# Batch 0's w_out product in split form, 24 matmuls of zeros ahead of TensorE's queue, and a new list of steps up to the first pair

## The chip, the cores and the metric

The kernel runs on one core of a Trainium2 chip. The metric is the device time of one execution in microseconds (us), lower is better. TensorE (PE) multiplies matrices, VectorE (DVE), ScalarE (ACT) and GpSimd (POOL) work on elements, and SyncE (SP) issues all transfers (DMA).

## The reference

Three stages follow one another. The first is an attention between 512 tokens and 32 state vectors per head, in both directions; the second a gated block with layer norm; the third a two-layer block. Cut to what matters:

```python
# x: [8 batches, 8 heads, 512, 64], state: [8, 8, 32, 64]
scores  = scale * x @ state.T;  a  = softmax(scores);  xread = a  @ state
scores2 = scale * state @ x.T;  a2 = softmax(scores2); sread = a2 @ x
x = concat([xread, sread]) as rows of 512        # 8 * (512 + 32) = 4608 rows
h = x @ w_in                                      # 512 -> 1024
solu = h * softmax(h)
ln = (solu - mean) / sqrt(var + 1e-6) * g_ln      # over the 1024
x = ln @ w_out                                    # 1024 -> 512
h = x @ w_in2;  g = max(0.01 * h, h);  out = g @ w_out2   # 512 -> 2048 -> 512
```

The weights come as 64-bit floats; the kernel narrows them itself.

## The kernel before, in words

**Stages.** Batches are worked on one by one through the first two stages. Per batch b: x is loaded (`x`), state is loaded (`z`) and transposed (`Z`), x is transposed (`T`), scores and their softmax run in both directions (`S`, `U`), the second direction is transposed and multiplied with x (`A`, `R`), the first is transposed (`B`). State times w_in is formed once (`Y` for batches 0 and 1, `W` for later pairs), so that `h` is the softmax times that product, followed by softmax, product and layer norm over 1024 columns. `t` transposes the result, four blocks to a PSUM bank, and `X` multiplies it with w_out into the rows of the next stage, which go to DRAM. The rows of `sread` of all batches are treated once, as a ninth batch (`G`, `N`, `t8`, `X8`). Behind that the third stage runs over pairs of batches: the first pair (`H`, `O`, with the ninth batch in `K`, `Q`) prepares the weights chunk by chunk, and the other three pairs follow a pattern that is repeated (`rest`, line 1253, token `F`). There the weights of w_out2 for later pairs are formed by GpSimd out of a loaded tile `wf` (`part_wo2`, line 766).

**Split form and plain form.** A product in split form takes each operand as a rounded high part and the rest as a low part, both of type fp32r, and adds three matmuls (`mm3`): high by high, high by low, low by high. In plain form (`mm1`) it is one fp32 matmul, which the trace shows as two records. `PLAIN_S = (0, 1)` names the batches whose attention and `h` are plain; `PLAIN_L = (0,)` (line 32) the batches whose product with w_out is plain. For those `tr` (line 563) writes one fp32 tile with a ScalarE copy per bank; for the others `split` makes a ScalarE cast to the high part and a VectorE subtraction for the low part. The product itself is `x2` (line 592). The plain one reads the narrowed w_out (`w_out_f`), the split one reads `w_out_hi` and `w_out_lo`, which `split_w_out` (tokens `p`, line 279) forms with a ScalarE cast and a GpSimd subtraction for each quarter.

**Narrowing.** `narrow` (line 198) turns a quarter of w_in (tokens `i`) or of w_out (tokens `o`, `narrow_w_out` in line 267) from 64 into 32 bits: one ScalarE step and four VectorE steps of 128x1024. w_out's quarters are then scaled by g_ln on ScalarE.

**Buffers.** The ring `ln` has four large buffers. They hold first the raw w_in (two) and the raw w_out (two); a buffer that comes free takes w_out_f, and later the transposed layer norm, two for a batch in split form and one in plain form. The four one-bank PSUM tiles are a ring too (`bank`), as are the three row buffers (`row`). x has one buffer `xn`, so x of the next batch can be loaded only behind `R` of the one before.

**The order.** It is written out by hand in `PROGRAM` (line 1356): a list of tokens, each of which advances one of the small generators above by one step (`stage`, line 1312). The first token `T0.0` issues the transposes, the second the eviction, and so on. Everything issued through `InOrder` keeps this order on its engine, and on SyncE's queue for transfers; so a step that waits holds back whatever stands behind it on the same engine. Only `make_identity`, which uses the engine directly, is not pinned. Constants are set by GpSimd ahead of the list (lines 153 to 178): the identity `ident`, `nhalf`, the zeroed state tiles `z0`, `z1`, the tile `stq` (128x2048, high and low part of the transposed state) and `stp`.

Of the kernel before, what the change touches and what calls it, by code (L numbers as in the profile page):

```python
# [64 lines left out]
def attn_solu_leaky_kernel(  # L65
# [1297 lines left out]
    Z2.0 h0.1 Y1.0.1 h0.1 Y1.0.1 o2 T1.0 h0.0 o0 T1.0 h0.1 h0.1 z3. T1.1 T1.1 h0.0 Z2.1 o2 S1.0
    h0.0 T1.2 T1.3 T1.2 S1.0 S1.0 T1.3 h0.0 h0.0 S1.0 S1.1 S1.0 S1.1 S1.1 h0.1 h0.0 U1.1 h0.2
    S1.1 h0.0 o0 h0.3 S1.0 U1.1 Z2.1 U1.0 U1.1 h0.0 h0.3 S1.1 h0.1 S1.1 U1.0 U1.0 h0.1 A1.0 A1.0
    A1.1 A1.1 h0.0 j1 t0.0.0 t0.0.0 U1.1 U1.1 h0.2 h0.1 t0.1.0 h0.3 t0.0.1 U1.0 U1.0 t0.1.0 h0.3
    h0.2 h0.3 j3 t0.0.1 R1 R1 B1.0 Z3.0 B1.1 h0.3 h0.2 h0.2 t0.1.1 h0.2 t0.1.1 h1.2 x2. R1 h0.3
    h0.3 h0.3 Z2.1 Z3.0 Z3.0 h1.2 h0.2 h1.0 R1 h0.3 t0.3.1 Z3.0 Z2.1 Z2.1 Z3.0 h0.2 t0.3.0 T2.2
    o3 T2.0 t0.3.1 h0.2 t0.3.0 T2.0 h0.2 t0.2.0 T2.1 h1.2 t0.2.0 o3 T2.0 T2.1 T2.1 o3 h1.0 h1.0
    p1 T2.2 t0.2.1 t0.2.1 T2.3 T2.2 j3 h1.2 T2.3 S2.0 S2.0 X0.1 h1.2 X0.1 h1.2 Z3.1 j0 j0 T2.3  # L1370
    S2.0 S2.1 h1.3 h1.0 Z3.1 h1.0 h1.0 S2.1 h1.1 j1 z4. S2.1 S2.1 o3 h1.1 h1.2 j1 h1.2 S2.0 Z3.1
    U2.1 W1.0.0 S2.1 o3 W1.0.1 h1.3 o3 o2 X0.1 U2.1 W1.0.0 j0 W1.0.1 h1.0 S2.0 U2.0 h1.3 W1.0.1
    X0.1 Z3.1 Z3.1 X0.1 w1.3 W1.0.0 X0.2 h1.3 h1.1 h1.0 X0.2 W1.1.0 W1.0.0 W1.0.1 W1.0.1 h1.0
    W1.0.0 W1.1.0 U2.0 h1.3 W1.3.1 U2.0 U2.1 W1.1.0 W1.1.0 X0.2 X0.2 X0.1 X0.0 X0.0 h1.2 W1.3.1
    W1.3.1 X0.2 X0.2 W1.3.1 h1.3 h1.3 h1.2 h1.0 t1.0.0 W1.3.1 U2.1 t1.0.0 t1.0.1 t1.0.0 z5. h1.1
    p1 S2.0 h1.1 X0.0 W1.1.0 U2.1 t1.0.1 X0.0 t1.0.1 U2.0 X0.0 S2.1 W1.3.0 W1.3.0 W1.3.0 U2.0
    X0.3 A2.0 A2.1 W1.3.0 W1.3.0 X0.3 A2.1 h1.3 t1.2.0 W1.1.1 A2.0 W1.1.1 h1.1 p2 h1.3 t1.2.1
    W1.1.1 t1.2.1 p3 X0.3 X0.3 h1.1 W1.1.1 B2.0 t1.2.0 t1.2.1 X0.0 w1.2 X0.3 h1.3 B2.1 R2 R2 x3.
    h1.1 B2.0 t1.2.0 B2.0 R2 B2.1 h1.1 W1.2.0 h1.1 W1.2.0 W1.1.1 B2.1 X0.3 t1.1.0 W1.2.1 W1.2.1
    R2 t1.3.0 t1.1.0 W1.2.0 t1.1.0 t1.3.0 W1.2.1 W1.2.0 W1.2.0 h2.2 W1.2.1 h2.1 W1.2.1 t1.3.1  # L1380
# [142 lines left out]
```

## Time and profile before

| | us |
|---|---|
| median of three runs | 1156.82 (1155.01 to 1158.55) |
| profiled execution, its own time | 1156.16 |
| its span, first to last instruction | 1154.4 |
| TensorE busy | 1128.9 (98%) |
| VectorE busy | 895.7 (78%) |
| ScalarE busy | 540.7 (47%) |
| GpSimd busy | 540.2 (47%) |

A span is measured within the profiled execution; its own time has some 1.8 us around the span. Busy time is a union of instructions; the mean of a group counts each instruction from its start to its end, and the next may start a little before that end. Tile names in a row stand as output<-inputs: `st` scores, `xt` transposed x, `zt` transposed state, `sw` and `sv` state times w_in, `h` and `e` the gated block, `tr` and `ln` its transposes, `x` the product with w_out, `wi`, `wo`, `wn` weights that are being narrowed.

### The profile page before, as it was taken

The page shows a single profiled execution, that of the slowest core. Times are in us where ns is not written, and L with a number is a line of the kernel's source. Part 1 is how long each engine was busy: PE and PEld are TensorE (multiplying, and loading weights), DVE is VectorE, ACT ScalarE, POOL GpSimd, SP SyncE. Part 2 cuts the span into 40 slices and gives each one's busy share as a digit, 9 for nine tenths or more (in the row PEclk, how much of TensorE's full clock was granted, in tenths as well). Part 3 has the DMA queues.
Part 4 walks back from the last instruction along what each step waited for, and adds up shares of the span by engine and source line. Part 5 has one row for each costly group of instructions (what it writes and reads, how often), then busy time and mean ns, then how long its engine had stood idle before and what let it go on. Part 6 is the DMA issues. An engine that isn't in the chain of part 4 may idle for free.

```text
span 1154.4 us, 16468 instructions
## 1 busy us (share of the span) xinstructions
PE 1128.9 (98%) x6192; PEld 945.8 (82%) x6192; DVE 895.7 (78%) x1406; ACT 540.7 (47%) x907; POOL 540.2 (47%) x411
## 2 busy tenths in 40 slices
...
GB/s 317 93 107 136 55 96 64 139 19 92 152 70 108 130 162 155 246 210 131 243 208 202 183 346 220 289 238 229 318 292 273 179 278 254 236 222 236 148 192 74
DMA packets 88376, 211.85 MB, mean 184 GB/s; under 512 B 41320, under 2 KB 49512, under 8 KB 79080
## 3 DMA queue, kind: packets, MB, share of 16 engines
...
## 4 chain that ended last, share of the span: by engine, by line
PE 89%; DMA 4%; DVE 3%; issue 1%; POOL 1%; ACT 0%; POOLq 0%; SPq 0%; DVEq 0%; ACTq 0%
PE x L51 17%; PE hX L51 14%; PE oX L51 10%; PE h L51 10%; PE o L51 8%; PE hY L51 7%; PE oY L51 5%; PE hZ L51 3%; PE tr L51 3%; PE sr L51 2%; PE oZ L51 2%; PE st L51 2%; PE sv L51 1%; DVE C L51 1%; PE sw L51 1%
## 5 line engine op out<-in xcount | busy, mean ns | idle before, releaser
L51 DVE TENSOR_TENSOR oacc<-oacc,oX 128x512 f32<-128x512 f32 x171 | 116.2, 683 | 52.9 <-PE oX L51 51.0
L51 PE MATMUL x<-ln,w_out_hi 128*128 128x512 f32 (+1 forms) x512 | 153.8, 384 | 0.0
L51 PE MATMUL hX<-xbT,w 128*128 128x512 f32 x576 | 149.9, 395 | 1.5 <-ACT C L51 1.2
L51 ACT COPY C<-hX 128x512 f32<-128x512 f32 x96 | 56.4, 587 | 171.1 <-PE hX L51 171.0
L51 PEld LDWEIGHTS hX<-xbT,w 128*128 128x128 f32 x576 | 103.4, 188 | 21.3 <-ACT C L51 1.6
L51 PEld LDWEIGHTS x<-ln,w_out_hi 128*128 128x128 f32 x512 | 92.2, 188 | 17.6
L51 PE MATMUL h<-sw,a1T 128*128 128x512 f32 x352 | 103.6, 436 | 0.0
L51 PE MATMUL x<-ln,w_out_lo 128*128 128x512 f32 (+1 forms) x256 | 97.2, 380 | 0.0
L51 POOL TENSOR_TENSOR gc<-C,gc 128x512 fp32r<-128x512 f32 (+1 forms) x43 | 69.3, 1614 | 50.2 <-ACT gc L51 25.5
L51 POOL TENSOR_TENSOR gb<-C,gb 128x512 fp32r<-128x512 f32 (+1 forms) x43 | 69.8, 1629 | 45.9 <-ACT gb L51 23.6
L51 DVE SCALAR_TENSOR_TENSOR C<-C 128x512 f32<-128x512 f32 (+1 forms) x88 | 82.7, 940 | 0.6
L51 PEld LDWEIGHTS h<-sw,a1T 128*128 128x128 f32 x352 | 64.1, 188 | 23.2 <-issue 11.0
L51 DVE TENSOR_TENSOR C<-C,hY 128x512 f32<-128x512 f32 x64 | 43.9, 686 | 43.7 <-ACT C L51 35.2
L51 DVE TENSOR_TENSOR oacc<-oacc,oY 128x512 f32<-128x512 f32 x93 | 63.3, 683 | 2.7 <-PE oY L51 2.0
L51 DVE TENSOR_TENSOR oacc<-oacc,o 128x512 f32<-128x512 f32 x70 | 45.7, 681 | 21.6 <-PE o L51 21.3
L51 PEld LDWEIGHTS x<-ln,w_out_lo 128*128 128x128 f32 x256 | 48.1, 188 | 9.8
L51 DVE TENSOR_TENSOR ln<-tr,ln 128x512 fp32r<-128x512 f32 x60 | 40.4, 684 | 17.9 <-ACT ln L51 17.5
L51 POOL TENSOR_TENSOR gb<-S,gb 128x512 fp32r<-128x512 f32 x27 | 44.6, 1656 | 16.8 <-ACT gb L51 8.1
L51 ACT CAST ln<-tr 128x512 fp32r<-128x512 f32 x60 | 34.5, 588 | 35.3 <-PE tr L51 35.2
L51 PE MATMUL hX<-xbB,w 128*128 128x512 f32 x192 | 50.9, 401 | 0.0
L51 POOL TENSOR_TENSOR gc<-S,gc 128x512 fp32r<-128x512 f32 x26 | 39.3, 1521 | 24.6 <-ACT gc L51 12.7
L51 PE MATMUL hY<-xbB,w 128*128 128x512 f32 x192 | 49.7, 394 | 0.4 <-DVE C L51 0.4
(696 smaller groups left out, 2801.8 us busy)
## 6 DMA issues: line engine op xcount, KB each, us to landing
...
```

What stands on the lines that cost most here:

```text
L51: done = call(*args, **kw)
```

## The change

It sets `PLAIN_L` to nothing: batch 0's product with w_out runs in split form as that of all others, and its transposed layer norm takes two `ln` buffers. It puts 24 matmuls of zeros, 128x512 of type fp32r into one PSUM bank, in front of TensorE's queue; they read the first quarter of `stq`, whose zeroing is moved ahead of the rest, while the identity, `nhalf` and the rest of `stq` are set behind. And `PROGRAM` is written anew from its first token to the start of `F`. In the new list the load of g_ln is the first transfer, the first two loads of w_in precede state, both others precede the second state, and x of batch 0's second half comes behind these; two `Y0.0` steps stand in front of `T0.2` and `T0.3`; the splits of w_out (`p`) stand in front of `X0.1` or within it; the order of the other steps differs in most places.

```diff
+WARM = 24
 PLAIN_S = (0, 1)
-PLAIN_L = (0,)
+PLAIN_L = ()
...
     ident = slot("ident", [P, P], F32, "ident")
-    make_identity(tc.nc, ident)
     nhalf = slot("nhalf", [P, 1], F32, "nhalf")
-    nc.gpsimd.memset(nhalf, -0.5)
...
     stq = slot("q7", [P, 2, NHP, 4 * BLK], F32R, "stq")
-    nc.gpsimd.memset(f32(stq), 0.0)
+    nc.gpsimd.memset(f32(stq[:, 0, :2, :]), 0.0)
+    warm = bank("warm")
+    zeros = stq[:, 0, :2, :].rearrange("p a b -> p (a b)")
+    for _ in range(WARM):
+        nc.tensor.matmul(warm, zeros[:, :P], zeros, start=True, stop=True)
+    drop("warm")
+    make_identity(tc.nc, ident)
+    nc.gpsimd.memset(nhalf, -0.5)
+    nc.gpsimd.memset(f32(stq[:, 0, 2:, :]), 0.0)
+    nc.gpsimd.memset(f32(stq[:, 1]), 0.0)
...
-            raws["w"] = slot(take("ln", "w_out_f", 4 + ND), [P, NF, DM], F32, "w_out_f")
+            raws["w"] = slot(take("ln", "w_out_f", 4 + ND * len(PLAIN_L)), [P, NF, DM], F32, "w_out_f")
...
 PROGRAM = """
-    a0 i0 i0 i0 i0 i0 z0. Z0.1 a1 x0.0 T0.0 Z0.0 a3 i1 i1 i1 Z0.0 Z0.0 z1. i1 T0.0 i1 T0.1 T0.1
-    a2 S0.0 x0.1 i3 Z0.1 Z1.1 i2 Z1.1 Z0.1 T0.3 Z1.1 T0.2 Y0.0.0 i3 i3 i3 T0.3 z2. i2 i2 i2 T0.2
-    i2 Z1.0 S0.1 Y0.0.0 S0.0 S0.0 Z1.0 Z1.0 j2 j2 b0 i3 S0.1 S0.1 o0 U0.0 U0.1 S0.0 b2 b3 o2
...
+    g a0 i0 i0 i0 a1 x0.0 T0.0 z0. i1 T0.0 T0.1 Z0.0 Z0.0 i0 a3 i0 a2 Z0.1 z1. T0.1 i1 i1 Z0.1
+    i1 Z0.1 i1 x0.1 z2. Z0.0 i3 i2 b0 b1 i3 b2 b3 i3 S0.0 S0.0 S0.0 S0.0 Y0.0.1 Y0.0.1 Z1.0 i3
+    Y0.0.0 i2 T0.2 i3 i2 Z1.0 T0.2 S0.0 i2 T0.3 T0.3 S0.1 U0.0 Z1.0 i2 Y0.0.0 Z1.1 S0.1 Y1.0.1
...
```

(The last lines are cut; some 2,100 tokens are in another order.)

## Rows read from the trace of the kernel before

**Rows 1.** The page, part 1: busy time, share of the span, instructions.
```profile
PE 1128.9 (98%) x6192; PEld 945.8 (82%) x6192; DVE 895.7 (78%) x1406; ACT 540.7 (47%) x907; POOL 540.2 (47%) x411
```

**Rows 2.** TensorE's waits in the span: us in total, times, longest.
```profile
PE zt L51 <- DMA z<-in_state: 6.9, 1, 6.9
PE xt L51 <- DMA xn<-in_x: 5.3, 5, 2.3
PE oX L51 <- POOL gc L51: 3.4, 2, 3.1
```

**Rows 3.** The chain of waits up to 180 us: start, us, what.
```profile
6.97 6.92 DMA raw_in<-in_moe_w_in
...
14.31 4.62 DMA xn<-in_x
...
76.18 1.41 PE st L51 x6
...
90.78 6.87 PE x L51 x16
...
141.30 8.40 PE x L51 x36
```

**Rows 4.** One stretch: length, busy of PE, PEld, DVE, ACT, POOL, clock, DMA.
```profile
7.17:78.00 70.83, 66.78 (x271) 38.81 (x271) 67.47 (x120) 49.01 (x94) 13.58 (x14) 1.00 0.57 171
```

**Rows 5.** Groups by form, 0 to 440 us: busy, mean ns, idle before.
```profile
L51 DVE TENSOR_TENSOR ln<-tr,ln 128x512 fp32r<-128x512 f32 x58 | 39.0, 684 | 15.9 <-ACT ln L51 15.6
...
L51 DVE SCALAR_TENSOR_TENSOR wi<-raw_in,wi 128x1024 uint32<-128x1024 uint32 x4 | 4.9, 1226 | 0.1
...
L51 POOL TENSOR_TENSOR w_out_lo<-w_out_f,w_out_hi 128x1024 fp32r<-128x1024 f32 x4 | 9.6, 2390 | 2.6 <-ACT w_out_hi L51 2.6
```

**Rows 6.** The timeline, 0 to 80 us: start, us, engine, operation, idle before.
```profile
1.74 1.81 POOL L51 MEMSET stq<- 128x2048 f32 x1
...
12.86 3.75 PE L51 MATMUL st<-xT_hi,stp 128*128 128x512 f32 x4 [0.17 <-issue]
...
16.76 1.20 ACT L51 ACTIVATE wi<-raw_in 128x1024 f32<-128x1024 f32 x1 [1.60 <-DMA raw_in<-in_moe_w_in]
...
21.40 1.88 PE L51 MATMUL st<-xT_hi,stp 128*128 128x512 f32 x4
...
45.06 1.22 DVE L51 SCALAR_TENSOR_TENSOR e(0, 1)_386<-h,e(0, 1)_386 128x1024 f32<-128x1024 f32 x1
46.20 0.09 DVE L51 DVE_READ_ACCUMULATOR e(0, 1)_386<-h,e(0, 1)_386 128x1 f32 x1
...
73.65 1.46 DVE L51 SCALAR_TENSOR_TENSOR xT_lo<-xt,xT_hi 128x512 fp32r<-128x512 f32 x2
```

**Rows 7.** SyncE's issue of g_ln, then two stretches as in rows 4.
```profile
20.22 0.53 SPq L51 DMA_DIRECT2D gln<-in_moe_g_ln  x1
...
24.00:26.00 2.00, 2.00 (x6) 0.93 (x5) 2.00 (x5) 1.30 (x4) 2.00 (x1) 1.00 1.04 426
...
30.00:32.00 2.00, 2.00 (x12) 1.44 (x11) 1.90 (x6) 2.00 (x4) 1.05 (x1) 1.00 1.15 363
```

**Rows 8.** The timeline near x of batch 4: SyncE's issues, TensorE.
```profile
165.68 0.92 SPq L51 DMA_DIRECT2D wi<-wsc  x2
168.84 7.42 SPq L51 DMA_DIRECT2D xn<-in_x  x4
...
181.15 1.20 PE L51 MATMUL xt<-ident,xn 128*128 128x128 f32 x9 [1.93 <-DMA xn<-in_x]
```

**Rows 9.** The hand-over: GpSimd's timeline, the chain, one stretch.
```profile
693.14 0.74 POOL L51 TENSOR_TENSOR wd<-wf 128x256 f32<-128x256 f32 x1 [8.55 <-DMA wf<-wf2s]
...
699.88 2.56 PE hX L51 x6
...
701.00:703.00 2.00, 2.00 (x8) 1.71 (x7) 2.00 (x3) 0.53 (x2) 2.00 (x2) 0.52 1.06 453
```

**Rows 10.** A group by form, 440 to 680 us, columns as in rows 5.
```profile
L51 DVE SCALAR_TENSOR_TENSOR wn<-raw,wn 128x1024 uint32<-128x1024 uint32 x28 | 41.9, 1503 | 0.5
```

More of the change, by code (lines that the diff above doesn't have):

```diff
@@ L1363 @@
[L1363 to L1380, printed above, removed]
@@ new lines @@
+    A1.0 A1.1 U1.1 t0.1.0 h0.2 t0.1.0 U1.0 U1.1 t0.1.1 U1.0 t0.1.1 t0.1.1 t0.0.0 R1 h0.3 R1
+    t0.0.0 h0.3 h0.3 Y1.0.0 h0.2 Z3.0 U1.0 R1 B1.1 B1.0 Y1.0.0 h0.2 h0.2 R1 j2 h0.3 x2. t0.0.1
+    t0.0.1 t0.0.1 o3 h0.2 h1.0 t0.1.0 o3 p1 h1.2 Z3.0 Z3.0 o3 Z3.0 h0.3 h0.3 Z3.0 p0 T2.0 T2.3
+    T2.1 T2.3 T2.1 j3 o3 h0.3 h0.2 h0.2 T2.3 h1.2 t0.3.0 h0.2 p2 T2.1 p2 t0.3.0 t0.3.0 T2.2 T2.2
+    T2.2 j2 h1.0 Z2.0 t0.2.0 S2.1 T2.0 T2.0 Z2.0 j0 j0 Z2.0 h1.2 Z2.0 Z2.0 S2.1 t0.2.0 S2.1
+    t0.2.0 t0.2.1 h1.2 h1.2 p0 S2.0 S2.0 W1.0.0 S2.1 j0 t0.3.1 j1 t0.3.1 h1.3 h1.3 h1.0 S2.0
@@ new lines @@
+    W1.1.0 R2 X0.0 t1.0.1 R2 h1.2 t1.0.1 W1.2.1 h1.3 W1.1.0 x3. h1.1 X0.3 R2 h1.1 z5. h1.3 B2.0
+    R2 t1.0.1 B2.0 X0.0 B2.1 B2.1 W1.2.0 h1.3 W1.2.0 h1.1 h1.1 X0.3 W1.2.1 W1.2.1 B2.1 W1.2.0
+    t1.3.1 t1.3.1 W1.2.0 W1.2.0 W1.2.1 W1.2.1 X0.3 X0.3 Z4.1 h1.2 h1.2 t1.3.1 h1.1 h2.2 T3.0
+    Z4.1 Z4.1 h1.1 Z4.1 h1.1 T3.0 X0.3 h2.2 Z4.1 T3.2 h1.1 t1.3.0 T3.3 T3.0 T3.3 h2.2 T3.3
+    t1.1.0 h2.1 t1.1.0 T3.2 t1.1.0 T3.2 t1.3.0 t1.3.0 T3.1 T3.1 h2.1 t1.2.1 t1.2.1 T3.1 t1.2.0
+    t1.2.0 h2.1 t1.2.1 t1.2.0 h2.1 t1.1.1 t1.1.1 S3.0 S3.1 h2.1 h2.2 X1.0 S3.0 S3.0 S3.0 S3.0
@@ new lines @@
+    h2.2 h2.3 h2.3 h2.1 h2.1 Z4.0 Z4.0 S3.1 S3.1 X1.0 h2.0 S3.1 h2.1 t1.1.1 Z4.0 h2.0 h2.3 X1.0
+    X1.0 S3.1 S3.1 Z4.0 X1.1 U3.1 S3.0 A3.1 U3.1 U3.1 U3.0 X0.3 U3.1 h2.0 X1.0 A3.0 U3.1 A3.0
+    B3.1 h2.1 h2.1 A3.1 X1.1 h2.2 B3.1 X1.1 B3.1 R3 t2.1.0 h2.0 h2.0 h2.2 h2.2 Z4.0 t2.1.1
+    t2.1.0 h2.2 U3.0 t2.1.0 U3.0 R3 h2.2 t2.1.1 U3.0 X1.1 X1.0 X1.1 x4. U3.0 h2.0 R3 R3 t2.1.1
+    h2.0 B3.0 X1.2 X1.2 B3.0 t2.2.0 Z5.0 Z5.0 Z5.0 Z5.0 Z5.0 t2.2.0 X1.2 h2.0 h2.3 X1.2 h2.0
+    T4.2 B3.0 t2.2.0 T4.0 h2.3 T4.3 X1.1 X1.2 h3.0 T4.2 T4.1 h2.3 T4.2 h2.0 T4.3 T4.1 T4.1 T4.3
@@ new lines @@
+    h3.0 t2.0.1 h3.0 t2.2.1 T4.0 h2.3 h2.3 h3.3 h3.0 h3.3 h2.3 h3.0 S4.1 h3.1 t2.2.1 h2.3 T4.0
+    t2.3.1 t2.0.1 t2.0.1 h3.3 w2.1 t2.3.1 t2.3.0 t2.3.1 t2.3.0 t2.3.0 h3.3 h3.1 S4.1 S4.0 X1.2
+    t2.2.1 S4.0 S4.0 X1.3 X1.3 h3.1 U4.1 S4.0 Z5.1 Z5.1 Z5.1 S4.1 U4.0 S4.1 h3.3 t2.0.0 t2.0.0
+    t2.0.0 S4.1 X1.3 h3.0 w2.0 X1.3 U4.0 W2.0.0 X2.1 S4.0 S4.0 h3.2 h3.2 h3.3 X2.1 X2.1 X1.3
+    S4.1 W2.0.0 W2.0.0 Z5.1 h3.0 h3.0 X2.1 Z5.1 h3.0 h3.1 h3.3 X2.0 X2.0 X2.0 U4.0 X2.0 W2.0.0
+    U4.1 U4.1 h3.1 W2.0.0 U4.0 U4.1 X1.3 X2.1 h3.0 h3.1 U4.0 h3.2 h3.3 X2.1 h3.1 W2.0.1 X2.0
@@ new lines @@
+    U6.1 X4.2 X4.2 h5.1 h5.1 Z7.1 h5.1 h5.2 w3.1 U6.1 t5.0.0 t5.0.1 t5.0.1 X4.2 U6.0 X4.2 Z7.1
+    Z7.1 t5.0.1 Z7.1 U6.0 S6.1 h5.3 h5.3 h5.3 W3.1.1 t5.0.0 t5.0.0 X4.1 h5.3 S6.1 h5.3 X4.1
+    W3.1.0 W3.1.0 W3.1.1 A6.1 A6.1 W3.1.0 U6.1 W3.1.0 h5.2 X4.1 X4.1 W3.1.0 X4.2 X4.1 W3.1.1
+    h5.1 X4.0 W3.1.1 X4.0 X4.0 W3.0.1 h5.2 h5.1 w3.3 h5.3 h5.3 h5.2 A6.0 h5.2 U6.1 W3.1.1 B6.1
+    U6.0 A6.0 U6.0 W3.0.1 W3.0.0 X4.1 X4.0 w3.2 W3.0.0 W3.0.0 X4.0 h5.3 R6 B6.0 R6 h5.1 W3.0.0
+    W3.0.1 W3.0.0 W3.3.0 h5.2 h5.2 h5.2 W3.0.1 W3.0.1 W3.3.0 X4.0 X4.3 W3.3.0 R6 W3.2.0 W3.2.0
@@ new lines @@
+    h6.2 U7.0 U7.0 h6.0 U7.1 U7.1 S7.1 S7.1 h6.2 S7.0 X4.3 X5.1 X5.0 U7.0 X5.2 U7.0 t6.0.0
+    t6.0.1 U7.1 U7.1 B7.1 h6.1 t6.0.0 h6.2 B7.0 S7.1 t6.0.1 B7.1 h6.1 B7.0 S7.1 h6.1 t6.0.1 X5.0
+    h6.1 X5.1 X5.2 h6.1 S7.0 B7.1 B7.0 X5.1 h6.2 h6.2 X5.1 h7.1 h7.1 t6.2.0 h6.3 X5.2 X5.1
+    t6.2.0 t6.2.0 A7.0 h6.1 h6.1 h6.1 h6.1 A7.0 h7.0 t6.0.0 X5.3 t6.2.1 t6.2.1 t6.2.1 X5.3 h7.1
+    h7.1 X5.1 X5.3 A7.1 A7.1 t6.1.1 h7.1 X5.3 X5.3 t6.1.0 w4.1 h7.0 h6.3 t6.1.0 t6.1.1 t6.1.1
+    X5.3 h7.0 h7.2 h7.2 h7.0 t6.3.0 h7.0 R7 t6.3.1 t6.3.0 t6.1.0 t6.3.0 h7.0 t6.3.1 h7.0 h7.0
@@ new lines @@
+    d2.1.0 K0 H0.1.4 H0.1.5 H0.1.4 O0.0.1.2 d2.1.0 d2.1.0 d2.0.3 d2.0.2 H0.1.6 d2.0.1 d2.1.0
+    O0.0.1.3 d1.1.4 d2.0.3 H0.1.1 d2.0.3 d2.0.3 O0.0.0.3 K0 K0 K1 K1 d2.0.2 H0.1.5 K0 H0.1.5
+    d3.0.0 d3.0.0 H0.1.7 d2.0.3 d1.0.5 H0.1.6 d3.0.0 d3.0.0 d3.0.0 H0.2.0 H0.2.1 K0 d2.0.3
+    O0.0.0.3 H0.2.0 H0.2.2 H0.2.2 O0.0.0.1 O0.0.0.1 H0.1.6 H0.1.5 H0.2.3 O0.0.0.2 H0.2.4 d3.0.3
+    d3.0.2 Q0.0 Q0.1 d3.0.3 d3.0.3 d2.1.5 K1 H0.2.4 H0.1.5 d2.0.4 H0.2.5 d3.0.1 Q0.0 K1 d3.0.2
+    H0.1.6 K2 H0.2.1 d3.0.3 K1 H0.2.4 H0.2.6 H0.2.5 d2.1.2 K1 H0.1.6 d3.0.4 H0.2.5 H0.3.0 d2.0.5
@@ new lines @@
+    K3 d3.1.0 d3.1.0 H0.3.7 H0.3.5 d5.0.0 d3.1.0 d5.0.3 d5.0.2 d5.0.3 H0.4.3 H0.4.4 H0.4.4
+    d5.0.3 O0.1.1.2 d3.1.0 H0.4.1 d3.1.5 d5.0.2 O0.2.0.3 d3.1.1 d5.0.1 d5.0.3 H0.3.5 O0.1.1.1 K3
+    H0.4.4 O0.2.0.3 d4.1.0 O0.2.1.2 d3.1.2 O0.2.1.1 O0.2.1.3 H0.4.5 d4.0.4 Q2.0 K4 H0.4.6
+    O0.2.1.3 d3.1.2 O0.2.0.1 O0.2.1.0 Q2.0 H0.3.6 d4.1.0 Q2.1 K3 d4.1.0 d5.0.3 O0.2.1.2 H0.3.6
+    d6.0.0 O0.2.0.1 d4.1.0 d4.1.0 O0.2.1.0 K4 K3 O0.2.0.2 K4 H0.4.6 Q2.1 O0.2.0.0 O0.2.0.2
+    H0.4.5 d4.1.1 H0.4.5 d5.0.3 d3.1.4 d4.1.5 K4 d5.1.0 O0.3.0.1 Q3.1 Q3.1 H0.3.6 O0.2.0.0
```

199 lines of the change are left out of this document (85 added, 114 removed).

## The prediction

> **What bounds the kernel now.** I read the busy shares first: TensorE (PE) is busy 98% of the span [rows 1], so either its work must shrink or one of its few waits must go. TensorE's list of waits comes next [rows 2]: 12.2 us at the very start, for state and x, and one of 3.1 us for GpSimd (POOL) as the largest later. Third, the chain of waits: DMA until x lands at 14.31 + 4.62 = 18.93 us, and from there TensorE nearly without a break [rows 3]. So a microsecond taken from TensorE's work behind 19 us is one of the end, as long as nothing else becomes late. The fourth view says what could: VectorE (DVE) is busy 67.5 of the 70.8 us between 7.17 and 78 [rows 4]. Two engines are nearly full there, and the change rewrites the order of both.
>
> **The product of batch 0 in split form.** Before, it is 64 records, two for each of 32 matmuls; 16 of them take 6.87 us in the chain, 0.429 each [rows 3]. The split form is 32 x 3 = 96 matmuls; 36 of another batch take 8.40 us, 0.233 each [rows 3]. 27.5 becomes 22.4: 5.1 us less TensorE work, on the path. VectorE gets eight subtractions ln<-tr,ln of 0.68 us [rows 5], 0.62 from start to start, 5 us in all. ScalarE's evictions stay one for one. The four splits of w_out move in front of the product: 4 x 2.39 us on GpSimd [rows 5], which works 13.6 of those 70.8 us, and four casts on ScalarE, which works 49.0 [rows 4]; they fit.
>
> **The 24 matmuls of zeros** wait for two short memsets and a quarter of one of 1.81 us [rows 6], so they begin near 2 us. At the start four matmuls of the scores take 3.75 us, later 1.88 [rows 6]: half the speed first. By these rows 24 matmuls, one pass each where a record of the scores has two, last 24 x 0.23 = 5.5 to 24 x 0.47 = 11.2 us and end between 7.5 and 13; I take 10, nearer to the slow row, which is that of an engine just started. The first x lands at 9.6. Bounds: 1.9 us gained on the first scores, 3.5 us lost if all run slow. I cost them at nothing: TensorE waits for w_in and x until 20 us with or without them. If that cover were gone they would cost those 3.5.
>
> **The start.** Two products of state and w_in (Y0.0, 1.72 us each) now precede the transposes that need the second half of x, so 3.4 us of work fill a wait. But that half comes later. The x load issued at 14.31 waited for the w_in load issued at 6.97 (landed at 13.89) [rows 3], which stands eight places ahead of it in SyncE's list. Counted so in the new list, the last quarter of x waits for the fourth w_in load, which reached ScalarE at 16.76 [rows 6], and lands near 20 instead of 18.93. At 20 us TensorE would be 3.4 - 1.0 = 2.4 us ahead.
>
> **VectorE's queue takes that lead away.** I compare one point: the scores of batch 2, first head group. Before, they run at 76.18 [rows 3], and the last VectorE step that they read ends at 73.65 + 1.4 = 75.0 [rows 6]. Counting VectorE's list up to there by its rows, each from start to start (a step of 1.22 us is followed after 1.14 [rows 6]): four narrowings of w_in at 3.7 us, 14.8; w_out's, 11.7; softmax of four score tiles in both directions, 7.7 and 9.2; layer norm of batch 0, 14.7; smaller steps, 6.5. That is 64.6. From 7.17 to 75.0 are 67.8, so 3.2 us were idle. In the new list the same scores have behind them 1.9 us more of w_out, five of the new subtractions (3.1) and two more of xT_lo (1.3): 70.9 us. The start moves too, as the load of g_ln now stands first: its issue takes 0.53 us, and at 28 to 32 us, where its 4-byte pieces go, the rate falls from about 426 to 363 GB/s for some 4 us, which is 0.5 us of transfer [rows 7]. I take 0.8 (bounds 0.5 and 1.0). For VectorE's idle I take 2 us, between 0.7 (what its first loads cost before 20 us) and 3.2. The scores come at 7.2 + 0.8 + 70.9 + 2 = 80.9. TensorE has 60.4 us of its list ahead of them, 59.4 before; with VectorE out of the way it would be there at about 75. So against before it is late by 80.9 - 76.2 - 1.0 = 3.7 us (2.2 to 5.1). Past this point VectorE's surplus shrinks; the next tight place, the first transposes of batch 1, has 1 us more room.
>
> **A wait that goes.** Near 179 us TensorE waits 1.93 us for x of batch 4: its four loads take 7.42 us to issue, just behind two loads of w_in [rows 8]. In the new list x of batch 4 stands directly behind the sums that free its buffer, no load of w_in is near, and 7.5 us of TensorE work lie between, where 6.6 to 7.3 sufficed for batches 2 and 3. I take the 1.9 off (bounds 0 and 1.9). For batch 2 the room falls from 6.6 to 5.7 us, but VectorE's lateness covers that.
>
> **The first pair and the hand-over** to the second keep their work; only the order changes. One wait is there: at 696 TensorE waits the 3.1 us for GpSimd [rows 2], which sat 8.55 us for a load of wf; behind it the granted clock is 0.52 (1.2 GHz) and six matmuls need 2.56 us [rows 9] instead of 1.4. Bounds: 4.3 us gained if it goes, 4.3 lost if it doubles. The new list ends again with the steps behind which that load is issued, so I leave it as it is.
>
> **Sum**, against the profiled execution's own 1156.16 us: 1156.16 + 3.7 - 5.1 - 1.9 = **1152.9**. The median of the runs shown is 0.7 higher, inside their spread of 3.5; I do not shift.
>
> **Rivals.**
> *The lead is kept.* If VectorE is not late (no idle, steps that overlap more), the whole gain comes: 1156.16 - 2.4 - 5.1 - 1.9 = 1146.8. For it: among TensorE's waits before there is none for VectorE in that stretch [rows 2]. Against: 70.9 us of listed work cannot pass in the 67 us that this asks.
> *GpSimd slows VectorE.* In the first pair VectorE's two-input step wn<-raw takes 1503 ns [rows 10], against 1226 on w_in [rows 5]: 23% more. By the same count GpSimd has 22.4 us of work in front of the product, 12.7 before; 10 us more x 23% = 2.3 us, and 1155.2. Against: the steps there read one input from PSUM as often as both from SBUF. The Trainium skill's "GPSIMD Engine Reference" (Key points) states that GpSimd shares its SBUF interfaces with VectorE and contends with VectorE steps that have two SBUF inputs. By that rule the splits moved forward are not free; no row of the stretch before 80 us shows it yet.
> *Slower.* TensorE and VectorE wait for each other by turns, because the list leaves neither a reserve: each microsecond that VectorE idles before the scores of batch 2 goes into the end. The gain is gone from 5.3 us of idle on; with 10 it is 1160.9. For it: 3.2 us of idle in the old list, and a clock that fell after a wait of 3.1 us. Against: that idle came late in the stretch.
> *The zeros do not raise the clock.* Then the first scores still take 3.7 us, and the sum stays, since a wait follows them: 1152.9 as well.
>
> **Chances.** Forecast with either state of the zeros 0.50 (own range 1150 to 1156), lead kept 0.15, GpSimd's contention or the wait for x staying (1155) 0.24, slower 0.11. A measurement of this kernel can tell about 0.3%, 3.5 us, from no change; faster means under 1153.3. 0.29 of the forecast's half lie there, with the first rival and a little of the second 0.45; same 0.45; slower 0.10. Eight in ten lie between 1147 and 1160: the lag's ends, the hand-over's bounds and the rivals but for their last tenth on each side.
>
> **What would show it.** Right: x<-ln,w_out_f gone and 96 more split records at 0.233; TensorE waits of 1 to 4 us for VectorE, or ScalarE behind it, between 28 and 81 us; the scores of batch 2 at 80 to 81; no wait for xn near 175; the first scores in 1.9 us. Wrong: scores of batch 2 before 77 (faster than forecast), VectorE idle over 5 us before 81 (no gain), or another wait near 690.

## The result, and the profile after

The changed kernel takes 1143.91 us (median of four runs, 1142.76 to 1144.52), the kernel before 1157.62: ratio 0.9884, 95% interval 0.9865 to 0.9903. That is 13.7 us by the medians and 12.4 by the two profiled executions (own time 1143.79 against 1156.16, span 1142.0 against 1154.4). The forecast was 1152.9 with a range from 1147: right in its sign, too small by 9, and outside its range.

The page after, part 1, as in [rows 1]:

```profile
PE 1126.7 (99%) x6248; PEld 956.6 (84%) x6248; DVE 899.8 (79%) x1414; ACT 538.9 (47%) x907; POOL 548.1 (48%) x413
```

TensorE's busy time falls by 2.2 us with the 8.3 us of zeros in it, so its own work takes 10.5 us less; matmuls that ran at the lower clock before count in that. Its list of waits after, as in [rows 2] (us in total, times, longest):

```profile
PE zt L52 <- DMA z<-in_state: 2.5, 2, 2.2
...
PE zt L52 <- DVE xT_lo L52: 0.9, 1, 0.9
...
PE xt L52 <- DMA xn<-in_x: 0.5, 2, 0.3
...
PE oX L52 <- POOL gc L52: 0.3, 1, 0.3
```

The wait for x of batch 4 (1.93 us of the 5.3 of [rows 2]) is gone, and that of 3.1 us for GpSimd at the hand-over is 0.3. Where along the span the time came from is read from the first start of four groups of TensorE (duration in ns min/median/max, first to last start in us). Before:

```profile
L51 PE MATMUL st<-xT_hi,stq x48: 389/396/482, 75.9 to 339.8; 128*128 128x512 f32 x48
L51 PE MATMUL hX<-xbB,w x192: 387/393/628, 442.2 to 1119.2; 128*128 128x512 f32 x192
L51 PE MATMUL oX<-shared,gc x108: 277/283/387, 695.5 to 1063.8; 128*128 128x256 f32 x108
L51 PE MATMUL oX<-misc,gc x180: 277/283/385, 717.3 to 1148.2; 128*128 128x256 f32 x180
```

After:

```profile
L52 PE MATMUL st<-xT_hi,stq x48: 387/396/503, 78.7 to 337.6; 128*128 128x512 f32 x48
L52 PE MATMUL hX<-xbB,w x192: 387/393/467, 436.7 to 1106.8; 128*128 128x512 f32 x192
L52 PE MATMUL oX<-shared,gc x108: 277/283/283, 689.0 to 1051.2; 128*128 128x256 f32 x108
L52 PE MATMUL oX<-misc,gc x180: 277/283/388, 705.9 to 1135.7; 128*128 128x256 f32 x180
```

At the scores of batch 2 the changed kernel is 2.8 us behind, 1.0 of it work that stood later before. At the first product of the first pair it is 5.5 us ahead, 0.9 of it two groups of transposes that now come later. Up to the first product that needs `gc` behind the hand-over it gains 1.0 more, and across the hand-over (689.0 to 705.9 instead of 695.5 to 717.3) 4.9. The last 1.0 comes behind it. Each list is read from one profile here; a second profile of the kernel before (e8) has its first product of the first pair at 446.6.

### The profile page after: what moved, and what is told of

Read it like the earlier page. It is cut to its first block, busy times and chain, and to the rows that moved or that the text cites. A ratio compares the mean times of both kernels' runs of the same rounds, so it can differ in the third digit from the quotient of the medians.

```text
span 1142.0 us, 16592 instructions
## 1 busy us (share of the span) xinstructions
PE 1126.7 (99%) x6248; PEld 956.6 (84%) x6248; DVE 899.8 (79%) x1414; ACT 538.9 (47%) x907; POOL 548.1 (48%) x413
## 4 chain that ended last, share of the span: by engine, by line
PE 92%; DVE 4%; DMA 2%; SPq 1%; issue 1%; ACT 0%; POOLq 0%; DVEq 0%; POOL 0%
PE x L52 16%; PE hX L52 15%; PE oX L52 11%; PE o L52 10%; PE h L52 9%; PE hY L52 8%; PE oY L52 6%; PE hZ L52 4%; PE oZ L52 3%; PE tr L52 2%; PE sr L52 2%; PE sv L52 2%; PE st L52 1%; SPq L52 1%; PE hs L52 1%; PE xt L52 1%
## 5 line engine op out<-in xcount | busy, mean ns | idle before, releaser
L52 PE MATMUL x<-ln,w_out_hi 128*128 128x512 f32 (+1 forms) x576 | 172.9, 384 | 0.0
L52 PEld LDWEIGHTS x<-ln,w_out_hi 128*128 128x128 f32 x576 | 104.1, 188 | 19.8 <-issue 0.5
L52 PE MATMUL x<-ln,w_out_lo 128*128 128x512 f32 (+1 forms) x288 | 109.3, 380 | 0.0
L52 DVE SCALAR_TENSOR_TENSOR C<-C 128x512 f32<-128x512 f32 (+1 forms) x88 | 77.6, 882 | 0.4
L52 PEld LDWEIGHTS x<-ln,w_out_lo 128*128 128x128 f32 x288 | 54.1, 188 | 10.6
L52 DVE TENSOR_TENSOR ln<-tr,ln 128x512 fp32r<-128x512 f32 x68 | 45.7, 682 | 17.0 <-ACT ln L52 16.6
L52 ACT CAST ln<-tr 128x512 fp32r<-128x512 f32 x68 | 38.7, 589 | 34.3 <-PE tr L52 34.2
L52 POOL TENSOR_TENSOR ee<-ee,sm 128x512 f32<-128x512 f32 x16 | 17.3, 1083 | 77.8 <-DVE sm L52 41.1
L52 PE MATMUL hY<-xbT,w 128*128 128x512 f32 x192 | 49.6, 393 | 0.0
## 6 DMA issues: line engine op xcount, KB each, us to landing
w<-w2s SPq DMA_DIRECT2D x24, 1792.0 KB, 10.5
```

What stands on the lines that cost most here:

```text
L52: done = call(*args, **kw)
```

## The experiments

Times are medians; a ratio is against the kernel before, run beside it on the same chip. The first runs set theory A (the gain sits in two places, the first two stages and the first pair with the hand-over) against rivals that put it into one place, or into the zeros.

### Where the gain sits: e1 and e2

The list is cut at the first `H0.0.0`, and the two parts are exchanged.

```diff
 e1: tokens before the first H0.0.0 as in the kernel before
-    H0.0.0 H0.0.0 H0.0.1 H0.0.2 D2.1 d0.0.5 X7.3
+    H0.0.0 D2.6 D2.6 D2.2 t8.0.0 t8.0.0 t8.0.1
...
 e2: the changed kernel, with the other order behind the first H0.0.0
```

> The kernel before, with its old list up to the first H0.0.0 (the first step of the first pair's product), and the new order for all that stands behind. Batch 0 stays plain, no zeros. Theory A (the gain has two places: the first pair with the hand-over behind it, 5.3 us, and the stretch near 826 us, 1.6 us, come from the order of the steps from H0.0.0 on; the rest comes from the first two stages): 1157.6 - 6.9 = 1150.7 us, no wait for GpSimd near 690, clock 1.00 there. Rival P (the wait at the hand-over is a matter of phase, set by when TensorE gets there and not by the order of the last steps): 1157.6, the wait of about 3 us is still there. Rival H (all of the gain is of the first two stages): 1157.6 and no change in the waits.

> The changed kernel with its list up to the first H0.0.0 and the old order behind. Theory A: the product in split form (5.1), the wait for x of batch 4 (1.9) and VectorE's lag at the start (-2.8) leave 4.2 us, so 1157.6 - 4.2 = 1153.4 us, and the wait for GpSimd of some 3 us at the hand-over is back. Rival P: the hand-over stays without a wait, 1145 us. Rival H: 1144 to 1146, though the waits of the first pair (0.4 and 0.4 us) are back.

e1: 1152.39, ratio 0.9963 (0.9948 to 0.9978), about 4 us, where 6.9 were expected; at the seam a new wait of 1.6 us for `ln` arose. e2: 1149.43, ratio 0.9931 (0.9911 to 0.9951), 8 us. In e2 the wait at the hand-over is back, and behind it the clock is down (TensorE's waits; then windows with length, busy of PE, PEld, DVE, ACT, POOL, clock, DMA):

```profile
PE oX L52 <- POOL gc L52: 3.2, 2, 3.0
```
```profile
690.00:694.00 4.00, 1.50 (x6) 1.41 (x7) 2.20 (x4) 0.83 (x2) 4.00 (x4) 0.74 0.94 321
694.00:698.00 4.00, 4.00 (x20) 3.35 (x19) 2.67 (x3) 2.04 (x3) 3.49 (x3) 0.83 1.05 446
```

In e1 the longest wait there is 0.3 us. Both parts gain: 0.0037 and 0.0069 of the time make 0.0106 of the 0.0116 that the whole change gives, and the new wait at e1's seam is more than the difference of 1.2 us. The wait at the hand-over follows the order behind `H0.0.0`, not the moment at which TensorE gets there: rivals P and H fall.

### The zeros: e3 and e11

```diff
 e3: the changed kernel
-WARM = 24
+WARM = 0
 e11: the kernel before
+    for _ in range(WARM):
+        nc.tensor.matmul(warm, zeros[:, :P], zeros, start=True, stop=True)
... (and the memsets in the new order)
```

> The changed kernel without the 24 matmuls of zeros; the memsets stay in the new order. Theory A, as forecast: the first scores take 3.7 us again, but TensorE waits for state until 19 us in any case: 1143.9 us. Rival V (VectorE's queue has no reserve, so what it gets later goes into the end): the first scores come 1.8 us later, VectorE waits for them, 1145.7. Rival C (all the work at half speed before 20 us is lost, 3.9 us by the sum of scores and transposes): 1147.8.

> The kernel before with the 24 matmuls of zeros and the new order of the memsets, and its own list. Five profiles of the old first stages have the scores of batch 2 at 75.9, 77.1, 77.9, 78.0 and 78.8, and where they are late, TensorE's granted clock between 20 and 40 us is 0.91 to 0.97. Theory Z (the zeros end 10 us before that and change nothing of it): ratio 0.999 to 1.001 and the same spread. Rival C (the zeros bring the clock up for good): the scores of batch 2 at 76, ratio 0.998.

e3: 1142.88 (1142.36 to 1143.31), ratio 0.9874; e11: ratio 0.9990 (0.9973 to 1.0007). The zeros give nothing in either list. TensorE's timeline shows why, first in the changed kernel, then in e3, then the first scores of e17, which is the changed kernel again (start, us; in brackets the wait before):

```profile
13.14 1.98 PE L52 MATMUL st<-xT_hi,stp 128*128 128x512 f32 x4 [0.25 <-ACT stp L52]
14.96 1.88 PE L52 MATMUL sw<-sw,stp 128*128 128x512 f32 x4
19.05 0.30 PE L52 MATMUL zt<-ident,z 128*128 128x128 f32 x1 [2.21 <-DMA z<-in_state]
```
```profile
13.38 3.20 PE L52 MATMUL st<-xT_hi,stp 128*128 128x512 f32 x4
16.41 1.88 PE L52 MATMUL sw<-sw,stp 128*128 128x512 f32 x4
19.25 0.30 PE L52 MATMUL zt<-ident,z 128*128 128x128 f32 x1 [0.96 <-DMA z<-in_state]
```
```profile
13.15 2.91 PE L52 MATMUL st<-xT_hi,stp 128*128 128x512 f32 x4
```

In e3 the first scores take 1.2 us longer than in the changed kernel's first profile, and the wait for state is 1.25 shorter: what they lose, the wait gives back. That first profile is the exception. In the six other profiles of this list's start with the zeros those scores take 2.91 to 3.57 us (e17 least, e10 most), in the four without them 3.02 to 3.77. In e11 the scores of batch 2 came at 78.5, not at 76 as rival C has it.

### The product: e4

```diff
-PLAIN_L = ()
+PLAIN_L = (0,)
```

> The changed kernel with PLAIN_L = (0,): batch 0's product with w_out plain again, all else as changed. Theory A: TensorE has 5.1 us more work on the path, VectorE 5.0 us less, 3.1 of it ahead of the scores of batch 2, where it is the one that is late (2.8 us by the traces): 1143.9 + 5.1 - 2 = 1147 us, and the scores of batch 2 come 2 to 3 us earlier. Rival S (the split form's gain is lost to VectorE: it gives back as much as TensorE gains): 1144. Rival L (VectorE isn't late anywhere, its steps overlap more): 1149 to 1150.6, and the scores of batch 2 stay at 78.7.

1146.94, ratio 0.9910 (0.9888 to 0.9931): 3.0 us more than the changed kernel, the number of theory A. The first product of the first pair comes at 441.2 instead of 436.7, 4.5 later; why less is left at the end, no run shows. The scores of batch 2 moved by 0.7 us only (78.0), though five subtractions were gone from VectorE's list ahead of them. That speaks against theory A's reason and against the forecast's sum over that list.

### VectorE's queue: e7 and e10

```diff
 e7, in narrow, for w_out's quarters 0 to 2
-        nc.vector.tensor_scalar(w, w, W_LOW, W_HIGH, ALU.max, ALU.min)
-        nc.vector.tensor_scalar(wu, wu, 3, 0x3FFFFFFF, ...)
 e10, for the same quarters; ScalarE then scales w
-        nc.vector.scalar_tensor_tensor(dst, lo, 29, wu, ALU.logical_shift_right, ALU.bitwise_or)
```

> The changed kernel without two of VectorE's steps in three of the four narrowings of w_out (clamp and shift): six steps of 128x1024 less, 4.0 us by their 0.66 us from start to start, all ahead of the scores of batch 2. Those values of w_out are not the reference's. Theory V as forecast (VectorE makes TensorE late by 3.7 us there): the scores of batch 2 at 75.0 instead of 78.7, 1143.9 - 3.7 = 1140.2 us. Theory V2 (it is late there, but by 1.8 us only, as the traces have it): the scores at 76.9, 1142.1. Rival N (VectorE is busy but not what TensorE waits for): 1143.9.

> The changed kernel without VectorE's last step in three of the four narrowings of w_out (the lower word is left out, so those values differ in their last bits); ScalarE scales what the step before it left. Three steps of 1.13 us less, of which two ran at 46.0 and 52.75, behind the point (44.9 us) from which the chain of waits runs over VectorE; the six steps left out before ran ahead of it. Theory V3 (VectorE sets the pace from 45 to 82 us and nowhere before): the scores of batch 2 at 76.5 instead of 78.7, 2 us less at the end, 1141.9. Rival N (VectorE isn't what TensorE waits for): 78.7 and 1143.9. Rival S (ScalarE, which is busy 54 of the 72 us from 20 to 92, is late at once): 77.7 to 78.7, 1143 to 1144.

1143.14 and 1144.18; the scores of batch 2 at 79.1 and 78.5. Neither 4.0 nor 3.4 us less on VectorE moves anything, so rival N stands so far: in e7 VectorE only waits 3.0 us for TensorE's `h` near 40 us. A sum over VectorE's queue, as the forecast made it, does not give the time of the scores.

### x of batch 4: e6

```diff
-    R3 Z4.0 Z4.0 Z4.0 Z4.0
+    R3 x4. w2.0 w2.1 Z4.0 Z4.0 Z4.0 Z4.0
... (the three tokens are taken out where they stood)
```

> The kernel before with the load of x of batch 4 moved directly behind the sums that free its buffer, and the two loads of w_in behind it. Theory A (the wait of 1.93 us near 179 us goes into the end one for one): 1156.6 - 1.9 = 1154.7, and no wait for x there. Rival: the load still ends too late, since its four parts take 7.4 us to issue wherever they stand, or another engine is late at once: 1156.6.

Ratio 0.9983 (0.9973 to 0.9994): 2 us, between 0.7 and 3.1. The wait is gone, as expected.

### The hand-over: e5 and e9

```diff
 e5, in the kernel before
-    /8.gA12 /8.t4 /8.hS4 O0.7.1.3 /8.gS3 /8.gS2 O0.7.1.1 O0.7.1.3 /8.ub /8.uc
+    /8.gA12 O0.7.1.1 /8.t4 /8.hS4 O0.7.1.3 O0.7.1.3 /8.gS3 /8.gS2 /8.ub /8.uc
 e9, in the kernel before
-    Q7.0 /7.uc /8.V /8.m6
+    Q7.0 /7.uc /8.V /9.U /8.m6
-            if np_ == 1:
+            if np_ == 1 and nc_ not in wf:
                 load_wf(nc_)
```

> The kernel before with two tokens moved in its last line before F: the sums and stores of the first pair's last two rows (second steps of O0.7.1.1 and O0.7.1.3) stand ahead of /8.gS3 and /8.gS2 instead of behind. Nothing else. Theory W (the third load of wf sits on SyncE behind the last store of the first pair, which waits for VectorE until 681.1; GpSimd, and behind it TensorE, waits for that load): the load goes out near 675 instead of 681.8, the wait near 696 goes with its slow clock, 1156.6 - 4.5 = 1152.1 us. Rival P (the new list cures the hand-over by something else, such as the order of the products or of GpSimd's steps): wait and time as before, 1156.6. Rival M (moving the sums forward makes VectorE late for the next products): slower by up to 2 us, 1158.6.

> The kernel before with one load moved: the third load of wf, which SyncE issues behind the last two stores of the first pair (at 681.8 us; with the stores moved forward it still went out only behind VectorE's step on misc and the last sum of the ninth batch), is issued behind /8.V, near 673. Nothing else. Theory W2 (the wait at the hand-over is this load's): GpSimd has wf by 685, the wait of 3 us near 696 and its slow clock go, ratio to before 0.9963 (-4.3 us). Rival O (the load earlier only lets GpSimd wait for something else, ScalarE's gc or a load of w that is now later, and the new list's gain in the first pair is the order of the products): ratio 0.999 to 1.001, a wait near 696 for another engine. Rival D (three more transfers at once slow the stores and the loads of w): slower, 1.002.

e5: ratio 1.0002 (0.9987 to 1.0017), no change. It moved the wrong tokens: the load of `wf` still stood behind VectorE's step on `misc` and behind the last sum of the ninth batch (`Q7.1`, the last token before `F`), as SyncE's queue in e5 shows:

```profile
682.98 0.32 SPq L51 DMA_DIRECT2D wt2s<-misc  x1
683.57 0.57 SPq L51 DMA_DIRECT2D out<-oacc  x1
684.25 1.16 SPq L51 DMA_DIRECT2D wf<-wf2s  x1
```

e9 moves the load itself: ratio 0.9947 (0.9926 to 0.9968), 6 us between 3.7 and 8.6. In its timeline the load goes out 8.8 us earlier than before, GpSimd (POOL) works on `wf` without a wait, and what it then waits for is ScalarE's part of `gc`:

```profile
672.94 2.83 SPq L51 DMA_DIRECT2D wf<-wf2s  x1
...
684.13 0.73 POOL L51 TENSOR_TENSOR wd<-wf 128x256 f32<-128x256 f32 x1
...
691.52 1.29 POOL L51 TENSOR_TENSOR gc<-C,gc 128x512 fp32r<-128x512 f32 x1 [4.44 <-ACT gc L51]
```

The windows there, in the kernel before and in e9:

```profile
696.00:700.00 4.00, 0.97 (x5) 0.97 (x6) 2.44 (x3) 1.37 (x3) 4.00 (x4) 0.94 0.82 306
700.00:704.00 4.00, 4.00 (x16) 3.29 (x16) 2.94 (x3) 1.53 (x3) 3.48 (x4) 0.64 1.06 448
```
```profile
696.00:700.00 4.00, 3.45 (x18) 2.96 (x19) 4.00 (x6) 1.99 (x4) 2.71 (x2) 1.00 0.92 343
700.00:704.00 4.00, 4.00 (x28) 3.64 (x27) 1.81 (x4) 1.41 (x3) 4.00 (x4) 1.00 1.07 448
```

TensorE is busy 3.45 of the first 4 us instead of 0.97, and the clock stays at 1.00 (2.4 GHz). From the first product with `gc` to the group at 717.3 (before) it is 21.8 us before, 17.75 in e9 (695.07 to 712.82) and 16.9 in the changed kernel, for the same matmuls in the same order. So one transfer's place in one queue makes 4.0 of the 4.9 us; of the rest, 0.6 is a wait for a load of `w`, up to 696.55, that e9 has and the changed kernel has not.

### The kernel before, profiled again: e8

> The kernel before, unchanged, profiled a second time, since its times spread over 8 us and those of the changed kernel over 2. If the start makes the spread: the first steps of batch 0 or the scores of batch 2 lie 2 us or more from where they lay (75.9), while the wait of 3 us near 696 is the same. If the hand-over makes it: the scores of batch 2 within 0.5 us and the wait near 696 another one.

Both expectations hold in part. TensorE's rows of e8 (its scores, x of batch 4, the window behind that):

```profile
L51 PE MATMUL st<-xT_hi,stq x48: 389/396/482, 78.0 to 344.3; 128*128 128x512 f32 x48
```
```profile
183.98 2.18 PE L51 MATMUL xt<-ident,xn 128*128 128x128 f32 x9 [2.72 <-DMA xn<-in_x]
```
```profile
184.00:188.00 4.00, 4.00 (x15) 3.56 (x16) 2.62 (x4) 2.17 (x4) 0.00 (x0) 0.57 0.00 1
```

The scores of batch 2 came 2.1 us later than in the first profile, the wait for x of batch 4 was 2.7 instead of 1.9 us, and behind it the clock was at 0.57. In eight profiles of the old first stages those scores lie between 75.8 and 78.8; in eight of the new list's (all but e13, e16 and e18) between 78.0 and 79.1. The kernel before ran between 1151.5 and 1161.5 us in all its runs, the changed one between 1142.2 and 1144.5.

### What holds TensorE before the scores of batch 2: e13, e16, e17, e18

```diff
 e13: narrow without clamp, shift and sign for w_out's last quarter
 e16: the same three steps moved (WARM = 0)
-    t0.1.0 o3 p1 ... Z3.0 o3 Z3.0 ... j3 o3 h0.3
+    S2.1 T2.0 T2.0 o3 o3 o3 Z2.0 j0
 e18: one split of w_out moved (WARM = 0)
-    h0.2 p2 T2.1 p2 t0.3.0
+    h1.2 Z2.0 Z2.0 p2 p2 S2.1
```

> The changed kernel without three of VectorE's steps (clamp, shift, sign; 2.4 us by their 0.6, 0.6 and 1.1 from start to start) in the narrowing of the last quarter of w_out, which run from 70 to 72.8 us. Those values of w_out are not the reference's. Theory V4 (VectorE holds TensorE only behind 70 us, where the chain of waits joins it and TensorE idles 1.9 us up to 80): the scores of batch 2 at 76.8 instead of 78.7, end 1.5 to 1.9 us earlier, 1142.2. Rival B (TensorE, ScalarE and VectorE are so level there that no single engine's work matters): 78.3 to 78.7, 1143.9.

> The changed kernel without zeros, and with the three steps of VectorE in the narrowing of w_out's last quarter (clamp, shift, sign; 2.4 us) moved behind the low part of x of batch 2, so behind the scores. The output is the reference's. Theory V4: the scores of batch 2 at 76.8 and 2 us less at the end, 1141. Rival M (VectorE has no room behind them either, it is busy 19.5 of the 20 us from 80 to 100, and the wait only moves): scores at 76.8, but the last x of batch 0 or the softmax of batch 2 is as much later, 1142.9.

> The changed kernel once more, beside e16: 1143.9 us, between 1142.4 and 1144.6, its own spread a quarter of that of the kernel before (8 us), because its first stages start from the same point whatever the clock does before 24 us (scores of batch 2 at 78.5 to 79.1 in five profiles of this list).

> The changed kernel without zeros, and with one split of w_out (both tokens of p2: ScalarE's cast and GpSimd's subtraction) moved behind the last step of Z2.0, so that GpSimd's 2.35 us no longer start at 74 us beside VectorE's step on e(0, 2). All of VectorE's steps stay. The output is the reference's. Theory G (GpSimd's step holds VectorE's up by 1.9 us, and TensorE waits for that): the step on e(0, 2) takes 0.8 us, the scores of batch 2 come at 76.8 instead of 78.7, end 1.5 to 2 us earlier, 1141 to 1141.4. Rival V (VectorE's queue as such): scores at 78.7, 1142.9. Rival M (the meeting moves to another step of VectorE, as the narrowing near 85 us, 2.15 us instead of 1.2 in the run with the plain product): scores at 76.8, 1142 to 1143.

e13: 1140.79, ratio 0.9861 (0.9841 to 0.9882), the scores at 76.7. The time is some 3 us below the changed kernel's, with intervals that overlap. Why these 2.4 us count when the earlier 4.0 did not, the timelines show. The changed kernel, GpSimd's split of w_out and VectorE, between two steps of TensorE:

```profile
66.06 0.66 PE L52 MATMUL tr<-ident,e(0, 0)_445 128*128 128x128 f32 x4 [0.57 <-ACT sw L52]
...
73.96 2.35 POOL L52 TENSOR_TENSOR w_out_lo<-w_out_f,w_out_hi 128x1024 fp32r<-128x1024 f32 x1 [2.18 <-ACT w_out_hi L52]
74.14 2.72 DVE L52 TENSOR_SCALAR e(0, 2)_584<-e(0, 2)_584,sn(0, 2)_540 128x1024 f32<-128x1024 f32 x1
...
76.78 0.68 DVE L52 SCALAR_TENSOR_TENSOR xT_lo<-xt,xT_hi 128x512 fp32r<-128x512 f32 x1
...
78.71 0.50 PE L52 MATMUL st<-xT_hi,stq 128*128 128x512 f32 x1
```

The same in e13, where VectorE gets to that step before GpSimd starts:

```profile
72.99 0.80 DVE L52 TENSOR_SCALAR e(0, 2)_584<-e(0, 2)_584,sn(0, 2)_540 128x1024 f32<-128x1024 f32 x1
73.85 2.37 POOL L52 TENSOR_TENSOR w_out_lo<-w_out_f,w_out_hi 128x1024 fp32r<-128x1024 f32 x1 [2.69 <-ACT w_out_hi L52]
```

A step of 0.8 us takes 2.72 when it starts 0.2 us into GpSimd's, and ends 0.55 behind it. The same step took 2.72 to 2.74 us in e3, e7 and e10: there, too, it met GpSimd's. e18 moves only the split and keeps all VectorE steps:

```profile
66.69 0.66 PE L52 MATMUL tr<-ident,e(0, 0)_421 128*128 128x128 f32 x4 [0.57 <-ACT sw L52]
...
74.77 0.80 DVE L52 TENSOR_SCALAR e(0, 2)_560<-e(0, 2)_560,sn(0, 2)_516 128x1024 f32<-128x1024 f32 x1
...
77.59 0.48 PE L52 MATMUL st<-xT_hi,stq 128*128 128x512 f32 x1
...
85.69 2.38 POOL L52 TENSOR_TENSOR wi<-sw,wi 128x1024 fp32r<-128x1024 f32 x1
85.96 3.19 DVE L52 SCALAR_TENSOR_TENSOR w_out_f<-raw_out,wo 128x1024 uint32<-128x1024 uint32 x1
```

The step is back at 0.80 and the scores come 1.1 us earlier. Counted from the same transposes (66.06 and 66.69) it is 10.9 us to the scores instead of 12.65, and 12.65 in e3 and e7 as well: 1.75 us of the 1.9 that theory G asks. But the next meeting, at 85.96, makes a narrowing step of 1.22 us last 3.19, and the time is 1142.95: rival M, and the same as e3 without zeros. e16: 1147.29, 4.4 us worse than e3. Moved behind the scores, the narrowing step met GpSimd too, the split of batch 2's state behind it came late, TensorE waited 4.1 us, and the clock fell to 0.50 (1.2 GHz):

```profile
78.44 3.25 DVE L52 SCALAR_TENSOR_TENSOR wo<-raw_out,wo 128x1024 uint32<-128x1024 uint32 x1
...
83.15 0.79 PE L52 MATMUL st<-xT_hi,stq 128*128 128x512 f32 x1 [4.07 <-DVE stq L52]
```
```profile
84.00:88.00 4.00, 4.00 (x13) 3.12 (x12) 3.92 (x7) 1.99 (x5) 1.89 (x1) 0.50 0.08 16
```

e17, the changed kernel again: 1143.52 (1142.16 to 1144.40), ratio 0.9880 (0.9856 to 0.9905).

### The gain rebuilt in the old list: e14 and e15

```diff
 e14: the kernel before with the edits of e6 and e9
 e15: e14, and
-PLAIN_L = (0,)
+PLAIN_L = ()
-    p1 T2.2
+    p0 p1 p0 p1 T2.2
-    o3 o2 X0.1 U2.1
+    o3 o2 p2 p3 p2 p3 U2.1
... (the other steps of p are taken out, one of X0.1 moved, eight steps of t0 added)
```

> The kernel before with its two moved loads at once: wf ahead of the last stores, x of batch 4 ahead of two loads of w_in. Plain product, no zeros, old order else. Theory T (the two waits are independent and go into the end): ratio 0.9947 x 0.9983 = 0.993, 1148.7 us where before is at 1156.7. Rival F (the second only moves the phase in which the first is met): 0.9947 to 0.996.

> The same with batch 0's product in split form: the splits of w_out stand where the first and the last of them can, two steps of X0.1 behind where they were. No zeros. Theory T: 5.1 us less than e14, ratio 0.9885, so the old list with two moved loads and the split product stands where the changed kernel stands (0.9884). Rival L (the new order gives something of its own, or hides the splits that here come late): 0.991 to 0.993, with waits of TensorE for GpSimd's w_out_lo between 80 and 100 us.

e14: 1148.77, ratio 0.9934 (0.9914 to 0.9954), as expected: two moved loads are 7.6 of the 13.4 us that a ratio of 0.9884 makes of 1157.6. e15: 1163.23, ratio 1.0042 (1.0025 to 1.0059), 14 us worse than e14 where 5 better were expected. TensorE's waits, and one window:

```profile
PE tr L51 <- DVE e(0, 1)_386 L51: 2.4, 1, 2.4
PE x L51 <- DVE ln L51: 2.0, 1, 2.0
PE x L51 <- POOL w_out_lo L51: 1.7, 1, 1.7
...
```
```profile
68.00:72.00 4.00, 4.00 (x21) 4.00 (x21) 3.96 (x8) 1.20 (x2) 2.67 (x2) 0.50 0.02 5
```

Put straight behind the casts, the subtractions hold VectorE's queue up (one, at 62.5 us, waits 2.3 us for ScalarE), TensorE waits by turns for VectorE and GpSimd, and behind the first wait the clock is at 0.50. The placing of the tokens was simple, so this is no bound on what the old order could do; it is one order in which the split form does not pay.

### A version better than both: e12

```diff
-WARM = 24
+WARM = 0
-    g a0 i0
+    a0 i0
-    b2 b3 i3
+    b2 b3 g i3
-    /7.uc O0.7.0.2
+    /7.uc /9.U O0.7.0.2
... (and the condition of load_wf as in e9)
```

> The changed kernel with three edits at once, as a version that could beat both: no zeros, the load of g_ln back behind those of w_out, and the third load of wf ahead of the last stores. VectorE starts at 7.2 instead of 7.6 us; the wait of 0.3 us for GpSimd at the hand-over goes. Theory: 1142.9 - 0.3 - 0.4 = 1142.2, ratio 0.987, not told apart from the kernel without zeros alone. Rival: g_ln arrives late for the first scaling of w_out, or the load of wf gets in the way of the last stores: 1144 to 1146.

1142.97 (1142.43 to 1144.15), ratio 0.9873 (0.9852 to 0.9894). With e3 and e18 it is the lowest of those that leave no work out; none of the three is told apart from the changed kernel.

## Why the prediction was wrong, step by step

**The product**: right. The chain after has 12 records of `x` in 2.76 us (below), 0.230 each, so 96 take 22.1 where 22.4 were expected, against 27.5 before. e4 puts 4.5 us on it at 440 us and 3.0 at the end.

```profile
94.42 2.76 PE x L52 x12
```

**The zeros at nothing**: right in the time, and for the reason given, a wait that follows (e3, e11); what it waits for is the second state, until 19.05. They end at 10.1, as taken. The sign "the first scores in 1.9 us" came in the first profile alone.

**The start, 2.4 us of lead**: wrong. x was there when it was wanted. But between the two `Y0.0` steps stands `Z1.0`, which needs the second state, and its load lands at 18.95 (the wait of 2.21 us at 19.05 above). Only one product filled the wait. Counted to the same work, the lead was 0.5 us: 19.05 + 57.1 us of work left, 1.0 of it new, against 19.57 + 56.1.

**VectorE's queue, 3.7 us**: wrong in its mechanism, and too large. The scores came at 78.7, not 80.9, which is 78.7 - 75.9 - 1.0 = 1.8 us of lag against that profile. That profile is an early one: against the middle of the eight with the old first stages, 77.5, the lag is 0.2. A queue that adds up to the whole stretch would have made e7 and e10 faster. What TensorE waits for is, for the most part, one meeting of VectorE with GpSimd at 74 us (e13, e18). That is the second rival's mechanism, 1.9 us where it priced 2.3, at a place that it didn't name: it met a one-input step of a kind that passes 1024 elements in 0.81 us. The Trainium skill's "SBUF — State Buffer" (SBUF: two separate sides) states of the port pair that both engines share that "the other fully blocks" until the first is done, for VectorE's fast modes as well as for two SBUF inputs. The trace agrees: 2.72 us is about the rest of GpSimd's step and most of its own 0.81. Which mode the step ran in, no view shows. The prediction had taken only the case of two inputs from its page, and found no row for it.

**x of batch 4, 1.9 us**: right (e6, 2 us).

**The hand-over "as it is"**: the step that failed most. The sentence was that the new list ends again with the steps behind which the load of `wf` is issued. It doesn't: `Q7.1`, whose sum and store stood last before, now comes early, and only the store of `misc` is in front, as SyncE's rows and GpSimd's first step behind show in the changed kernel:

```profile
672.92 0.33 SPq L52 DMA_DIRECT2D wt2s<-misc  x1
673.30 1.15 SPq L52 DMA_DIRECT2D wf<-wf2s  x1
...
681.77 0.73 POOL L52 TENSOR_TENSOR wd<-wf 128x256 f32<-128x256 f32 x1 [6.48 <-DMA wf<-wf2s]
```

From the load's issue to the first product that needs `gc` it is 15.7 us (673.3 to 689.0) instead of 13.7 (681.8 to 695.5), and it lands after 8.3 us instead of 11.3: 5.0 us more room for a wait of 3.1. The load in the chain before:

```profile
681.78 11.29 DMA wf<-wf2s
```

The wait and its slow clock [rows 9] go: of the 4.9 us across the hand-over 3.1 are the wait and 1.8 are matmuls (18.7 us of them before, 16.9 after). e9 alone gives 3.7 to 8.6 at the end. The prediction had bounded this term by 4.3 us either way and taken nothing; it had not followed SyncE's queue through the last twenty tokens.

**The sum**, with what was measured: 1152.9 - 1.9 (lag 1.8 for 3.7) - 4.9 (hand-over, for nothing) = 1146.1. In the profile of before TensorE also idled 0.4 and 0.4 us near 635 and 641 and 1.6 between 812 and 832, in that of after nowhere there: 1143.7, against 1143.79. That it meets so well is in part luck, as both profiles are single ones. Those last 1.6 us came and went among the profiles of either list, so they are not shown to be the change's.

**The rivals.** "The lead is kept" (1146.8) was nearest in its number and had no part in it. "Slower" did not come, but its mechanism did in e15 and e16. The range ended at 1147 because the hand-over's gain was given little weight, though a full gain there was inside its bounds.
